# A fused spectral filter and feed-forward kernel: last transform stage placed by the chunk that needs it, filter sign moved to the prologue, half of batch 2's products by DMA exchange

## The chip, the cores and the metric

The kernel runs on one core of a Trainium2 chip. The metric is the device time of one launch in microseconds; lower is better. Times quoted as runs are launches timed on the device; the profile is one further execution recorded by the hardware profiler.

## The reference

Eight sequences of 3008 positions and 256 channels are filtered in the frequency domain, and the result goes through a two-layer network with a leaky ReLU.

```python
# x [8, 3008, 256], filt_r and filt_i [1505, 256], w_in [256, 2048], w_out [2048, 256]
X = np.fft.rfft(x, axis=1)
Y = X * (filt_r + 1j * filt_i)[None, :, :]
y = np.fft.irfft(Y, n=3008, axis=1).reshape(8 * 3008, 256)
h = y @ w_in
return np.maximum(0.01 * h, h) @ w_out
```

All inputs and the output are float32; the kernel computes its matmuls in float16 with float32 sums.

## The kernel before

**The transform.** The length 3008 is split into 94 x 32. For each sequence (called a batch, b = 0 to 7) the filter is four stages of matmuls with constant matrices. Each stage is cut into groups, and each group's matmuls fill one PSUM bank.

- Stage 1 (`s1_group`, matmul L218, 16 groups): transform over the 94 positions. ScalarE copies the bank out (for three quarters of batch 1's groups VectorE does), and SyncE's queue (SP) stores every second group to a DRAM scratch tensor `dz1` (L223). `t1_load` (L228) brings it back with rows and partitions exchanged, into a ring of four buffers `z1`.
- Stage 2 (`s2_group`, L264, 12 groups): transform over the 32 positions, with the twiddle factors in the matrix, and then the product with the filter. `fa_sb` holds the real part of the filter on all 128 partitions, `fb_sb` the imaginary part. Partitions 0 to 63 hold real rows and 64 to 127 imaginary ones, so that the product needs the halves exchanged. In general VectorE forms p2 = ps x fb (L273), two DMAs of 64 partitions each exchange its halves into p3 (L274, L275, on SP), VectorE forms p1 = ps x fa (L276), and GpSimd (POOL) adds p1 + p3 into y (L278). For batch 1 VectorE instead writes p3 directly with two operations of 64 partitions (L270, L271), so no DMA is needed. The tags p1, p2 and p3 have two buffers each, y has four.
- Stage 3 (`sa_group`, L284, 12 groups): inverse over the 32 positions, copied out by ScalarE (L286), stored to `dz2` (L288), and brought back by `t2_load` (L233) into the ring of four buffers `z2`.
- Stage 4 (`sb_group`, L302, 16 groups, two for each of the eight row blocks h): inverse over the 94 positions, copied by ScalarE (L294) into `yt`, the network's input.

Batch 0 goes through a prologue of its own (`first_s1` to `first_sb`), which uses VectorE transposes in the place of DRAM. There the upper half of `fb_sb` is a copy of the lower half (`upper`, L370), and the sign of the exchanged product is carried by the constant `inv2x`. Batch 1 takes the sign from a -1.0 in L270. After batch 1 the upper rows are negated in place (L569), and later batches need no sign.

**The network.** The 24064 rows are cut into 47 chunks of 512. `moe1` (L438) multiplies a chunk with w_in, and ScalarE applies the leaky ReLU (L443). In the first four chunks and the last one, the second product is `plain` (L541); in the others it is a seven-product scheme on quarters (`product`, L489), with VectorE sums of inputs (L466) and outputs (L513 to L533). Both use `out_banks`, two PSUM banks. `store` (L478) writes the output rows from SP's queue.

**The order.** Nothing reorders the work by itself. Every piece is put with a time on one heap and is issued in order of these times, to in-order engines and queues. One chunk has eight time units (`SL = 8`): its 16 `moe1` steps are half a unit apart, and the products of the chunk before are spread between them. `plan` gives each transform group its time: stage 1 at `s1 + s1_step * g`, stage 2 at `s2 + s2_step * g`, stage 3 `lag` later, stage 4 at `sb + sb_step * g`. The loads of x for the next batch go on POOL's queue at `s1 + xl + x_step * g`. The groups of all batches are then sorted and kept at least `GAP = 0.6` apart. The turned loads are placed three units ahead of their stage, but not sooner than 1.7 units after the last group of the stage before it. Steps that follow a group use `soon(delay, ...)`: the exchange DMAs one unit after stage 2, the POOL addition 3 units after it (1.2 in batch 1).

The transform groups share a ring of two PSUM banks (`single`, after one has been given to `out_banks`): a group waits until the group two places before it has been read out.

A stage 4 group of block h of batch b must come before the chunk that first reads the block, `QT * (8 * b + h) // CH` with QT = 376 and CH = 512; an assertion holds the plan to that.

Of the kernel before, what the change touches and what calls it, by code (L numbers as in the profile page):

```python
# [11 lines left out]
P = 128  # L12
FP16 = mybir.dt.float16
FP32 = mybir.dt.float32
AL = mybir.AluOpType
# [11 lines left out]
def _build_np_constants(N):  # L27
    n1, n2 = np.arange(N1), np.arange(N2)
    h = N2 // 2

    k2 = np.concatenate([np.arange(h), np.arange(N2 - 1, h - 1, -1)])

    sg = np.where(k2 < h, 1.0, -1.0)[None, :]
    th = 2 * np.pi * np.outer(n2, k2) / N2
    co, si = np.cos(th), np.sin(th)

    fwd1 = np.zeros((P, P))
    fwd2 = np.zeros((P, NC, P))
    inv1 = np.zeros((P, N2, N1))
    inv2 = np.zeros((P, P))  # L40

    for s, (qr, qi) in enumerate(((0, 2), (1, 3))):
        k1 = NC * s + np.arange(NC)

        cr, ci = (slice(64 * i + s, 64 * i + 64, 2) for i in range(2))
        r, i = (slice(Q * q, Q * q + Q) for q in (qr, qi))
        ang = 2 * np.pi * np.outer(n1, k1) / N1
        fwd1[:N1, qr * Q : qr * Q + NC] = np.cos(ang)
        fwd1[:N1, qi * Q : qi * Q + NC] = -np.sin(ang)
        for c in range(NC):  # L50
            t = th + 2 * np.pi * n2[:, None] * k1[c] / N
            fwd2[r, c, cr], fwd2[i, c, cr] = np.cos(t), np.sin(t)
            fwd2[r, c, ci], fwd2[i, c, ci] = -np.sin(t) * sg, np.cos(t) * sg

        w = np.where((k1 == 0) | (k1 == N1 // 2), 1.0, 2.0)[:, None] / N1
        for j in n2:
            t = ang.T + 2 * np.pi * j * k1[:, None] / N
            inv1[qr * Q : qr * Q + NC, j, :] = w * np.cos(t)
            inv1[qi * Q : qi * Q + NC, j, :] = -w * np.sin(t)
        inv2[cr, r], inv2[ci, r] = co.T, -(si * sg).T  # L60
        inv2[cr, i], inv2[ci, i] = si.T, (co * sg).T
    inv2 /= N2

    inv2x = np.concatenate([inv2[64:], -inv2[:64]], axis=0)
    small = np.stack([fwd1, inv2, inv2x], axis=1)

    fwd2t = fwd2.reshape(4, Q, NC, P).transpose(1, 0, 2, 3).reshape(P, NC, P)
    inv1t = inv1.reshape(4, Q, N2, N1)[:, :NC].transpose(1, 0, 2, 3).reshape(4 * NC, N2, N1)
    fwd2 = fwd2.reshape(P, FP, NC // FP, P).transpose(1, 0, 2, 3)
    return tuple(np.ascontiguousarray(t).astype(np.float16) for t in (fwd2, inv1, small, fwd2t, inv1t))  # L70
# [3 lines left out]
def kernel(  # L74
# [9 lines left out]
    nc = tc.nc  # L84
    B, N, D = x.shape
# [5 lines left out]
    CH = 512  # L91
    NCHUNK = TOK // CH
    assert NCHUNK * CH == TOK
    SL = 8
    NCH = NCT // 2
    QT = 4 * N1
    W0 = 4
    GAP = 0.6
    LANDED = 1.7
    SUMS = (0.9, 1.9, 2.9, 3.9)  # L100

# [11 lines left out]
    fa_sb = cpool.tile([P, NC, D], FP16, name="fa_sb")  # L113
    fb_sb = cpool.tile([P, NC, D], FP16, name="fb_sb")
# [21 lines left out]
    def bank(kind, n, w):  # L136
        of = wide if kind == "ph" else single
        t = of[turn[kind] % len(of)]
        turn[kind] += 1
        return t[:, : n * w].rearrange("p (n w) -> p n w", n=n)  # L140
# [5 lines left out]
    def at(time, f):  # L146
        clock["n"] += 1
        heapq.heappush(work, (time, clock["n"], f))

    def soon(delay, f):  # L150
        at(clock["now"] + delay, f)
# [3 lines left out]
    fwd1, inv2, inv2x = (small_sb[:, i, :] for i in range(3))  # L155
# [104 lines left out]
    def s2_group(b, g):  # L260
        def go():
            ps = bank("pf", 2, D)
            for j in range(2):
                nc.tensor.matmul(ps[:, j, :], f2_sb[:, 2 * g + j, :],  # L264
                                 z1[g // 2 % 4][:, 2 * (g % 2) + j, :],
                                 start=True, stop=True)
            fa, fb = fa_sb[:, ds(2 * g, 2), :], fb_sb[:, ds(2 * g, 2), :]
            p1, p2, p3 = (scrp.tile([P, 2, D], FP32, tag=f"p{i}", name=f"p{i}_b{b}_g{g}") for i in (1, 2, 3))
            if b == 1:
                nc.vector.scalar_tensor_tensor(p3[0:64], ps[64:P], -1.0, fb[64:P], AL.mult, AL.mult)  # L270
                nc.vector.tensor_tensor(p3[64:P], ps[0:64], fb[0:64], AL.mult)  # L271
            else:
                nc.vector.tensor_tensor(p2[:], ps, fb, AL.mult)  # L273
                soon(1, lambda: nc.sync.dma_start(p3[0:64], p2[64:P]))  # L274
                soon(1, lambda: nc.sync.dma_start(p3[64:P], p2[0:64]))  # L275
            nc.vector.tensor_tensor(p1[:], ps, fa, AL.mult)  # L276
            ys[(b, g)] = y1 = ypp.tile([P, 2, D], FP16, tag="y", name=f"y_b{b}_g{g}")
            soon(1.2 if b == 1 else 3, lambda: nc.gpsimd.tensor_tensor(y1[:], p1[:], p3[:], AL.add))  # L278
        return go

    def sa_group(b, g):
# [14 lines left out]
    def sb_group(b, g, copy):  # L296
        h, dt = g // 2, g % 2

        def go():
            ps = bank("pf", 4, N1)  # L300
            for j in range(4):
                nc.tensor.matmul(ps[:, j, :], z2[h % 4][:K4, j, ts(dt, P)], i1_sb[:K4, 4 * h + j, :],  # L302
                                 start=True, stop=True)
            quad_copy(h, dt, ps, copy)
        return go
# [3 lines left out]
    act, dve = nc.scalar.copy, nc.vector.tensor_copy  # L309
# [59 lines left out]
    def upper(hf, t, copy):  # L369
        copy(t[64:P, :, ts(hf, DH)], t[0:64, :, ts(hf, DH)])  # L370


    def keep_warm(n):
        for _ in range(n):
# [4 lines left out]
    g = 0  # L379
    for (n0, nn), fill in zip(first_parts, (4, 3, 1, 14)):  # L380
        while nn:
            n = 2 if nn % 4 or n0 >= N2 - 4 else 4
            first_s1(n0, n, two[n // 4], (dve, act)[g % 2])
            n0, nn, g = n0 + n, nn - n, g + 1
        keep_warm(fill)
    t1_part(0, 0, True)(), t1_part(0, 1, True)()
    upper(0, fa_sb, act), upper(0, fb_sb, dve)
    first_s2(0, 8, 8, "ph", True)
    t1_part(0, 2, True)()
    first_s2(0, 0, 8, "ph")  # L390
# [6 lines left out]
    t1_part(0, 3, True)()  # L397
    first_s2(0, 20, 4, "pf")
    upper(1, fa_sb, act)
    upper(1, fb_sb, dve)  # L400
    keep_warm(4)
    first_s2(1, 8, 8, "ph", True)
    first_s2(1, 0, 8, "ph")
# [12 lines left out]
    for g in range(8, 16):  # L416
# [6 lines left out]
    out_banks = [t[:].rearrange("p (a t d) -> p a t d", a=2, t=2)  # L423
                 for t in (psp_last, po_ps.rearrange("p a d -> p (a d)"))]
# [43 lines left out]
    done = {"products": 0}  # L468
# [68 lines left out]
    def plain(ci):  # L537

        def one(tj, ct):
            po = out_banks[tj % 2].rearrange("p a t d -> p (a t d)")[:, :D]  # L540
            nc.tensor.matmul(po, gts[ci][:, ct, ts(tj, P)], w_out_sb[:, ct, :],  # L541
                             start=(ct == 0), stop=(ct == NCT - 1))
            if ct < NCT - 1:
                return
            ot = outp.tile([P, D], FP32, tag="ost", padded_shape=[P, 6 * P], name=f"ost_c{ci}_t{tj}")
            (nc.vector.tensor_copy if ci < W0 else nc.scalar.copy)(ot[:], po)
            soon(0.5, lambda: store(ci, tj, ot[:]))
        return [lambda tj=tj, ct=ct: one(tj, ct) for tj in range(4) for ct in range(NCT)]

    groups, loads = [], []  # L550

    def plan(b, s1, s1_step, s2, s2_step, lag, sb, sb_step, xl, x_step):
        for g in range(16):
            groups.append((s1 + s1_step * g, 1, b, g, s1_group(b, g, dve if b == 1 and g % 4 < 3 else act)))
            if g % 2 and b + 1 < B:
                at(s1 + xl + x_step * g, lambda n0=2 * g - 2: x_load(b + 1, n0, 4))
        for c in range(6):
            loads.append((s2 - 3, 1, b, c, t1_load(b, c)))
        for g in range(12):
            groups.append((s2 + s2_step * g, 2, b, g, s2_group(b, g)))  # L560
            groups.append((s2 + lag + s2_step * g, 3, b, g, sa_group(b, g)))
        for h in range(8):
            loads.append((sb - 3, 3, b, h, t2_load(b, h)))
        for g in range(16):
            groups.append((sb + sb_step * g, 4, b, g, sb_group(b, g, act)))

    for i, (o, i0, i1) in enumerate(wt_sums):
        at(10 + 0.5 * i, lambda o=o, i0=i0, i1=i1: nc.vector.tensor_tensor(o, i0, i1, AL.subtract))
    at(32, lambda: nc.vector.tensor_scalar(fb_sb[64:P], fb_sb[64:P], -1.0, None, AL.mult))  # L569
    at(26, lambda: nc.sync.dma_start(i1_sb[:K4], i1t_d.ap()))  # L570
    plan(1, 0.3, 0.55, 13, 1.25, 3.3, 36.4, 2.94, 4, 1.6)
    plan(2, 13, 1.55, 43.5, 2.6, 6, 82.5, 2.94, 11, 2.2)
    plan(3, 42, 1.75, 75, 3.75, 6, 129, 2.94, 4, 2.94)
    for b in range(4, B):
        z = 47 * b
        plan(b, z - 121, 2.94, z - 69.5, 3.92, 6.5, z - 12, 2.94, 4, 2.94)

    last, when = -1, {}
    for time, stage, b, g, f in sorted(groups, key=lambda v: v[0]):
        last = max(time, last + GAP)  # L580
        when[stage, b, g] = last
# [3 lines left out]
    for time, stage, b, c, f in loads:  # L585

        after = when[stage, b, 15 if stage == 1 else 11] + LANDED
        at(max(time, after, place.get((stage, c % 4), 0)), f)
# [50 lines left out]
```

## Time and profile before

| what | value |
|---|---|
| runs | 761.75, 763.34, 763.74 us (median 763.34) |
| profiled execution | 761.49 us; span 759.7 us from its first to its last instruction |
| instructions | 18968 |
| TensorE matmul busy | 741.3 us (98%), granted clock 0.996 |
| ScalarE busy | 562.4 us (74%) |
| VectorE busy | 490.6 us (65%) |
| POOL busy | 169.2 us (22%) |
| DMA | 111.71 MB, 147 GB/s in the mean |

In the profile, PE is TensorE's matmuls, PEld its weight loads, DVE VectorE, ACT ScalarE. A row of the timeline gives start, duration, engine, line, operation, output<-inputs and shapes, and in brackets the idle time of the engine just before and what ended it. "x16" says that so many like instructions are merged. A row of the busy time by window gives the stretch, its length, and for each engine its busy time and instructions; then the granted TensorE clock, the DMA engines' busy share and GB/s. Matmuls are pipelined, and the recorded ends are modelled, so that records of successive matmuls overlap.

### The profile page before, as it was taken

What the parts mean: (1) busy time and instruction counts of PE and PEld (TensorE: products, weight loads), DVE (VectorE), ACT (ScalarE), POOL (GpSimd) and SP (SyncE); (2) the same over time, 40 slices, a digit from 0 to 9 for tenths busy, and PEclk for the clock granted to TensorE, in tenths of its full rate; (3) what the DMA queues carried; (4) which work ended last, traced back from release to release, by engine and by line L of the source; (5) the groups of instructions that cost most, each with busy time, mean ns of one, the idle gap of its engine ahead of it and who ended that gap; (6) DMA issues with size and microseconds to landing.
All of it is one profiled execution on the core that took longest, in us unless ns stands there. A gap on an engine that the chain in (4) does not pass through costs nothing.

```text
span 759.7 us, 18968 instructions
## 1 busy us (share of the span) xinstructions
PE 741.3 (98%) x7829; PEld 529.4 (70%) x7829; DVE 490.6 (65%) x665; ACT 562.4 (74%) x755; POOL 169.2 (22%) x171
## 2 busy tenths in 40 slices
PE   8899989999899999999999999999999999999997
PEld 3556657667577777877778777787677777777776
DVE  5866645767566687766766776677577676555561
ACT  4876777788687877777877877878777777666763
POOL 4703431242312221212223212212211210000000
PEclk9999999999999999999999999999999999999999
DMA  9996776777775578566775655544553433211012
GB/s 187 245 208 159 166 173 178 197 180 196 193 209 148 118 202 219 137 144 157 194 193 136 163 166 165 149 136 119 149 174 102 121 86 105 57 54 54 28 47 67
DMA packets 118726, 111.71 MB, mean 147 GB/s; under 512 B 16160, under 2 KB 92576, under 8 KB 118448
## 3 DMA queue, kind: packets, MB, share of 16 engines
q1 hardware_dynamic: 103776, 94.02, 41.9%
q0 software_dynamic: 14864, 16.49, 15.6%
q8 instruction: 61, 1.00, 0.5%
q14 instruction: 25, 0.20, 0.1%
HBM read 57.48 MB, written 50.33 MB: 142 GB/s over the span
## 4 chain that ended last, share of the span: by engine, by line
PE 75%; DMA 2%; DVE 1%; ACT 0%; SPq 0%; issue 0%; DVEq 0%
PE ph L438 35%; PE pf L489 16%; PE po_ps L489 16%; PE pf L302 2%; PE pf L218 2%; PE pf L264 2%; PE pf L284 2%; DMA dz<-big 1%; DMA big<-dz 1%; PE pf L541 0%; PE po_ps L541 0%; ACT gt_c L443 0%; SPq L478 0%; DVE p_b_g L273 0%; DVE ost_c_h L513 0%
## 5 line engine op out<-in xcount | busy, mean ns | idle before, releaser
L443 ACT ACTIVATE gt_c<-ph 128x1024 f16<-128x1024 f32 x376 | 385.4, 1025 | 141.8 <-PE ph L438 133.2
L438 PE MATMUL ph<-yt,w_in_sb 128*128 128x512 f16 (+7 forms) x1728 | 447.4, 351 | 0.7 <-ACT yt L294 0.7
L489 PEld LDWEIGHTS <-gt_c 128*128 128x128 f16 x2688 | 194.5, 98 | 90.3 <-issue 1.3
L278 POOL TENSOR_TENSOR y_b_g<-p_b_g,p_b_g 128x512 f16<-128x512 f32 x84 | 116.9, 1392 | 440.8 <-DMA p_b_g<-p_b_g 311.1
L489 PEld LDWEIGHTS <-big 128*128 128x128 f16 x2016 | 144.5, 98 | 62.1 <-issue 1.0
L438 PEld LDWEIGHTS <-w_in_sb 128*128 128x128 f16 x1728 | 138.3, 98 | 19.0 <-issue 0.9
L273 DVE TENSOR_TENSOR p_b_g<-pf,fb_sb 128x512 f32<-128x512 f32 x72 | 49.6, 689 | 44.5 <-PE pf L264 24.5
L221 ACT CAST big<-pf 128x512 f16<-128x512 f32 x100 | 58.2, 582 | 13.2 <-PE pf L218 11.6
L489 PE MATMUL po_ps<-wt_sb,gt_c 128*128 128x128 f16 x672 | 67.6, 219 | 0.3 <-DVE ost_c_h L513 0.3
L489 PE MATMUL pf<-wt_sb,gt_c 128*128 128x128 f16 x672 | 67.2, 219 | 0.3 <-DVE ost_c_h L513 0.2
L489 PE MATMUL pf<-w_out_sb,gt_c 128*128 128x128 f16 x672 | 64.3, 219 | 0.0
L489 PE MATMUL po_ps<-wt_sb,big 128*128 128x128 f16 x672 | 63.8, 219 | 0.0
L489 PE MATMUL po_ps<-w_out_sb,gt_c 128*128 128x128 f16 x672 | 63.8, 219 | 0.0
L294 ACT CAST yt<-pf 128x376 f16<-128x376 f32 x117 | 55.1, 474 | 11.3 <-PE pf L302 9.1
L489 PE MATMUL pf<-wt_sb,big 128*128 128x128 f16 x672 | 63.5, 219 | 0.0
L276 DVE TENSOR_TENSOR p_b_g<-pf,fa_sb 128x512 f32<-128x512 f32 x84 | 57.3, 682 | 0.6 <-POOL y_b_g L278 0.2
L466 DVE TENSOR_TENSOR gt_c<-gt_c 128x2048 f16<-128x2048 f16 x42 | 55.6, 1324 | 1.1
L466 DVE TENSOR_TENSOR big<-gt_c,big 128x2048 f16<-128x2048 f16 x42 | 55.9, 1332 | 0.0
L286 ACT CAST big<-pf 128x512 f16<-128x512 f32 x84 | 49.0, 583 | 5.8 <-PE pf L284 4.6
L466 DVE TENSOR_TENSOR big<-gt_c 128x2048 f16<-128x2048 f16 x42 | 52.1, 1240 | 0.2 <-ACT gt_c L443 0.2
L466 DVE TENSOR_TENSOR big<-big,gt_c 128x2048 f16<-128x2048 f16 x42 | 51.5, 1226 | 0.0
L541 PEld LDWEIGHTS <-gt_c 128*128 128x128 f16 x320 | 31.2, 98 | 18.5 <-issue 1.2
(85 smaller groups left out, 665.5 us busy)
## 6 DMA issues: line engine op xcount, KB each, us to landing
dz<-big SPq DMA_DIRECT2D x98, 256.0 KB
p_b_g<-p_b_g SPq DMA_DIRECT2D x144, 128.0 KB
out_dram<-ost_c_h SPq DMA_DIRECT2D x114, 128.0 KB
big<-dz SPq DMA_DIRECT2D x42, 256.0 KB
big<-dz SPq DMA_DIRECT2D x56, 192.0 KB
x_sb<-in_x_dram POOLq DMA_DIRECT2D x41, 192.0 KB, 4.5
out_dram<-ost_c_t SPq DMA_DIRECT2D x14, 128.0 KB
x_sb<-in_x_dram POOLq DMA_DIRECT2D x2, 768.0 KB, 10.0
```

The costliest lines, as they stand in the source:

```text
L218: nc.tensor.matmul(ps, fwd1[:N1], x_sb[:N1, ds(2 * g, 2), :], start=True, stop=True)
L221: copy(st[:, ds(2 * (g % 2), 2), :], ps)
L273: nc.vector.tensor_tensor(p2[:], ps, fb, AL.mult)
L276: nc.vector.tensor_tensor(p1[:], ps, fa, AL.mult)
L278: soon(1.2 if b == 1 else 3, lambda: nc.gpsimd.tensor_tensor(y1[:], p1[:], p3[:], AL.add))
L286: nc.scalar.copy(st2[h % 4][:, ds(2 * (g % 2), 2), :], ps)
L294: copy(yv, ps.rearrange("p c a -> p a c"))
L438: nc.tensor.matmul(ph[:, j, ds(t - ci * CH, e - t)], w_in_sb[:, dt, ts(ct, P)], yt[:, dt, ds(t % N, e - t)], start=(dt == 0), stop=(dt == ...
L443: nc.scalar.activation(gts[ci][:, ds(2 * g, 2), :], ph, AF.Lrelu)
L466: nc.vector.tensor_tensor(o, i0, i1, op)
L489: nc.tensor.matmul(po[:, t], a()[:, c, ts(t, P)], w[:, c, :], start=(c == 0), stop=(c == NCH - 1))
L541: nc.tensor.matmul(po, gts[ci][:, ct, ts(tj, P)], w_out_sb[:, ct, :], start=(ct == 0), stop=(ct == NCT - 1))
```

## The change

- The prologue's copy into the upper half of `fb_sb` becomes a multiplication by -1 (`minus`); the later negation (L569) is gone, and `inv2x` has the opposite sign in its second half.
- In batch 1, the even groups of stage 2 keep the direct products, now with a plain `tensor_tensor` in the place of the scaled one. The odd groups use the DMA exchange as other batches do, with the POOL addition 2.6 units after stage 2.
- A stage 4 group is placed at its planned time or, where that is earlier, 3.5 units (first of a block's two groups) or 1.5 units (second) before the chunk that needs the block.
- `plain` takes its output bank by the count of products made. The count is read when the step is issued, after all the product lists have been made; it is 295 then, so that the first tile of a plain chunk uses the second bank.
- The plan's numbers change for batches 1, 2 and 4 to 7.

```diff
-    inv2x = np.concatenate([inv2[64:], -inv2[:64]], axis=0)
+    inv2x = np.concatenate([inv2[64:], inv2[:64]], axis=0)
...
+    EXG = 0
...
-            if b == 1:
-                nc.vector.scalar_tensor_tensor(p3[0:64], ps[64:P], -1.0, fb[64:P], AL.mult, AL.mult)
+            if b == 1 and g % 2 == EXG:
+                nc.vector.tensor_tensor(p3[0:64], ps[64:P], fb[64:P], AL.mult)
                 nc.vector.tensor_tensor(p3[64:P], ps[0:64], fb[0:64], AL.mult)
             else:
                 nc.vector.tensor_tensor(p2[:], ps, fb, AL.mult)
...
-            soon(1.2 if b == 1 else 3, lambda: nc.gpsimd.tensor_tensor(y1[:], p1[:], p3[:], AL.add))
+            soon(1.2 if b == 1 and g % 2 == EXG else 3 if b > 1 else 2.6, lambda: nc.gpsimd.tensor_tensor(y1[:], p1[:], p3[:], AL.add))
...
+    def minus(o, i):
+        nc.vector.tensor_scalar(o, i, -1.0, None, AL.mult)
...
-    upper(0, fa_sb, act), upper(0, fb_sb, dve)
+    upper(0, fa_sb, act), upper(0, fb_sb, minus)
...
-    upper(1, fb_sb, dve)
+    upper(1, fb_sb, minus)
...
-            po = out_banks[tj % 2].rearrange("p a t d -> p (a t d)")[:, :D]
+            po = out_banks[(done["products"] + tj) % 2].rearrange("p a t d -> p (a t d)")[:, :D]
...
-            groups.append((sb + sb_step * g, 4, b, g, sb_group(b, g, act)))
+            due = SL * (QT * (8 * b + g // 2) // CH)
+            groups.append((min(sb + sb_step * g, due - 3.5 + 2 * (g % 2)), 4, b, g, sb_group(b, g, act)))
...
-    at(32, lambda: nc.vector.tensor_scalar(fb_sb[64:P], fb_sb[64:P], -1.0, None, AL.mult))
...
-    plan(1, 0.3, 0.55, 13, 1.25, 3.3, 36.4, 2.94, 4, 1.6)
-    plan(2, 13, 1.55, 43.5, 2.6, 6, 82.5, 2.94, 11, 2.2)
+    plan(1, 0.3, 0.55, 12.8, 1.25, 3.3, 37, 2.8, 4, 1.6)
+    plan(2, 13, 1.55, 43.5, 2.6, 5.5, 84.2, 2.8, 13, 2.3)
...
-        plan(b, z - 121, 2.94, z - 69.5, 3.92, 6.5, z - 12, 2.94, 4, 2.94)
+        plan(b, z - 121, 2.94, z - 69, 3.92, 6.5, z - 11.6, 2.94, 4, 2.94)
```

## The prediction

> **What bounds the kernel now.** The page came first, then busy time by window, then TensorE's waits and, around each long one, the timeline.
>
> ```profile
> PE 741.3 (98%) x7829; PEld 529.4 (70%) x7829; DVE 490.6 (65%) x665; ACT 562.4 (74%) x755; POOL 169.2 (22%) x171
> ```
> ```profile
> 39.00:120.00 81.00, 78.03 (x512) 48.30 (x510) 44.37 (x72) 57.75 (x74) 22.85 (x25) 1.00 0.77 178
> 120.00:210.00 90.00, 85.50 (x931) 60.46 (x928) 61.69 (x85) 71.30 (x100) 26.21 (x27) 1.00 0.76 188
> 210.00:740.00 530.00, 528.79 (x5976) 389.53 (x5974) 352.90 (x474) 401.60 (x535) 96.57 (x88) 1.00 0.49 133
> ```
>
> After the span, the first column is TensorE: from 210 to 740 us it is idle for 1.2 us, from 39 to 210 for 7.5 us. TensorE is in order, so only its idle time can shrink. Its records overlap, so I took each start-to-start interval less the median of its kind (216 ns for 512 columns, 56 ns for the L489 products). From 39 us to the end 12.4 us of excess remain, nearly all at these places:
>
> ```profile
> 203.32 0.33 PE L489 MATMUL po_ps<-w_out_sb,gt_c 128*128 128x128 f16 x3
> 206.26 0.35 PE L302 MATMUL pf<-i_sb,big 96*128 96x94 f16 x4 [2.61 <-DMA big<-dz]
> ```
> ```profile
> 113.61 0.35 PE L302 MATMUL pf<-i_sb,big 96*128 96x94 f16 x4 [1.89 <-DMA big<-dz]
> ```
> ```profile
> 166.75 0.38 PE L438 MATMUL ph<-yt,w_in_sb 128*128 128x512 f16 x1 [0.69 <-ACT yt L294]
> ```
> ```profile
> 748.48 1.91 PE L541 MATMUL pf<-w_out_sb,gt_c 128*128 128x256 f16 x16 [0.52 <-DVE ost_c_h L513]
> ```
>
> By excess: 2.78 us where batch 2's last stage waits for its first turned load, 2.05 where batch 1's does, 0.85 where chunk 8 waits for batch 1's yt, 0.85 at 542.5 (batch 7's stage 2, its load late), 0.68 at the end (the plain product wants the bank that the last product's VectorE addition is leaving), 1.72 in seven waits of batch 1 (one row above all: the two-bank ring still held by VectorE), 1.04 at 143.3 (ring, VectorE late), 0.59 at batch 1's first load; the rest small.
>
> The chain of waits gives the largest:
>
> ```profile
> 196.48 0.87 ACT gt_c L443
> 197.35 6.22 DMA dz<-big
> 203.59 2.63 DMA big<-dz
> ```
>
> The store to DRAM takes 6.22 us, the load back 2.63. And batch 1's products:
>
> ```profile
> L270 DVE SCALAR_TENSOR_TENSOR p_b_g<-pf,fb_sb x12: 692/693/694, 59.3 to 97.9; 64x512 f32<-64x512 f32 x12
> L271 DVE TENSOR_TENSOR p_b_g<-pf,fb_sb x12: 683/683/685, 60.0 to 98.7; 64x512 f32<-64x512 f32 x12
> L276 DVE TENSOR_TENSOR p_b_g<-pf,fa_sb x12: 692/692/692, 60.7 to 99.4; 128x512 f32<-128x512 f32 x12
> ```
>
> Half the partitions cost the full time. A direct group holds its bank 2.5 us from its matmul, an exchanged one (two operations) 1.9.
>
> **The skill.** "VectorE: DVE Perf Modes", The perf-mode tier table, puts tensor_copy and tensor_scalar in one tier on 16-bit SBUF data. The trace agrees: the 64x3072 copies take 996 ns, the 64x6144 negation 1873. "DMA: Bandwidth & Descriptors", Anatomy of one DMA, gives a fixed cost of about 2 us. The exchange's second issue to its POOL addition takes 1.9 us at least, median 3.6 and at most 5.8 in batch 2: the fixed part is there, and more under load. The same page, Issuing engines are not separate DMA queues, says that they share the 16 engines. In agreement, three x loads (about 580 KB) are on POOL's queue at 104-110, just when batch 1's store takes 4.5 us.
>
> **The change, part by part.** The order of TensorE's work follows from the plan's numbers (due times, then the 0.6 spacing), so I listed it for both versions; listed so, the old order fits the trace matmul for matmul. "Distance" below is TensorE work between two points, without waits.
>
> 1. Negation. L370 on VectorE becomes a multiplication by -1, twice, at 996 ns either way (bounds -0.1, +0.1); L569's 1.87 us at 101.2 goes, VectorE being idle around it. L270's scalar_tensor_tensor becomes tensor_tensor, 693 to 683 ns. The sign of inv2x is data. Zero.
>
> 2. Batch 2's last stage: plan 82.5 to 84.2, lag 6 to 5.5. Last stage-3 group to first stage-4 group was 8.08 us apart plus 2.78 waiting, so the chain needs 10.86. The new distance is 12.08. The load (at start - 3, now 81.2) moves past SP's intervening work, but still ahead of the store's landing. -2.8; bounds -2.8 and -0.5. The shorter lag cuts stage 2 to 3 of group 11, already 0.42 late, by 0.17: +0.2.
>
> 3. Placement by chunk. For group 9 of batch 1 the distance to chunk 8 grows from 0.57 to 1.06 us (crowding eats the rest), so 0.85 becomes about 0.35: -0.5. Elsewhere the least leads are 1.8 us (batch 4) and 2.1 (batch 2); evacuation took 0.85 to 1.6 from the matmul. Zero; at worst +0.5.
>
> 4. Batches 4 to 7: stage 2 later by 0.5, stage 4 by 0.4. Batch 7's load was issued at 539.89 behind output stores on SP. It stays behind them, but its matmul is 0.82 us later in the order: -0.8. Batch 5's load moves past the stores at 2.8 into a chunk; it had 8.4 us of lead against some 3, so it hides. Other SP meetings may open: 0 to +1.5, I take 0.
>
> 5. Plain banks. At the end the parity frees the first tile: -0.7. In the first chunks it makes chunk 3's last tile share the first product's bank. That tile's copy ends at 119.26, the product starts at 119.08: +0.25.
>
> 6. x loads of batch 3: start +2.1 units, step 2.3. Two of the three at 104-110 leave batch 1's store window. I take -0.4 from the 2.05; bounds -1.0, 0. Their users are 6 units later, so their delay hides. Batch 1's stage 2 at 12.8 arrives 0.1 us earlier at its load: +0.1.
>
> 7. Exchange in six odd groups. VectorE saves 6 x 0.69 us; of the seven ring waits those behind odd groups go, while direct groups 4, 6, 8 and 10 keep the 2.4 us distance that cost about 0.28: 1.1 instead of 1.72, -0.6. Added are 12 DMAs of 128 KB on SP, issued in 1.1 us a pair; SP's plan point (+1 unit, about 2 us) is after the product is ready at 1.2, so nothing queues behind a waiting exchange for long. POOL's addition waits instead, and behind it x loads and the next direct addition (about 5 us of slack before). The chain is 0.48 to VectorE, 0.69, issue 1.16, landing, addition 1.27 and handover: 3.7 us plus landing. Batch 2 shows 5.85 to 12.3, median 7.6. Distances in batch 1 are 7.7, 9.0, 10.2, 9.0, 8.7 and 6.3 us (groups 1 to 11). Group 11 waits whenever landing exceeds 2.6 us; over batch 2's twelve values the mean excess is 1.2. Its successor's distance is unchanged, so this adds to the 2.05. Groups two apart share p1, so VectorE waits for POOL when landing exceeds about 4; with group 1 that is some 0.7. +1.9; bounds 0 and +6.
>
> Sum: -2.8 + 0.2 - 0.5 - 0.8 - 0.7 + 0.25 - 0.4 + 0.1 - 0.6 + 1.9 = -3.35 us, from the profiled span of 759.7 to about 756.3. That execution was timed at 761.49, the lower end of the runs; from the median 763.34 the same loss gives 760.0.
>
> **Rivals.** *The exchange becomes the bound* (slower): all odd chains at 10 us, inside batch 2's values, cost 2.3 + 1.0 + 0 + 1.0 + 1.3 + 3.7 = 9.3 us on TensorE against 5.3 of gains: +4, 767. For it: batch 1 has the tightest distances and DMA at 77%. Against: the distances were 2.6 to 5.3 us longer than the direct chain, and five of six exceed batch 2's median. It decides from a mean chain of about 9 us.
> *The wait only moves* (no change): batch 2's store is slowed by traffic moved beside it, or SP reaches the load late, and only 1 us of 2.8 comes back, with the exchange at its estimate: -1.5, 761.8. For it: 6.2 us against batch 1's 4.5 shows how the store varies.
> *The exchange hides*: landing near 2 us, as in batches 4 to 7 (median 2.0). Then item 7 is -0.6 and the gain 5.2: 758.1. Against: DMA is 77% busy here, 49% there.
> *The change doesn't do what it says*: placement by chunk hardly binds, since the spacing sets most groups; that costs item 3 alone.
>
> **How the numbers follow.** About 0.3%, or 2.3 us, can be told from no change. The forecast (gain 2.3 to 5) has 0.57, the hidden exchange 0.10, the moved wait 0.21, the slower rival 0.12. The likeliest gives 760.0. The range 757.2 to 763.8 runs from the hidden exchange plus half of item 6's bound past the moved wait to the start of the slower rival; about 0.05 lies below and 0.12 above. Faster 0.67, same 0.21, slower 0.12.
>
> **What would show it.** Right: no wait over 0.5 us at batch 2's first L302; none at the last L541; batch 1's odd chains of 6 to 9 us and a wait of about 1 us before its last L284; SP's load for batch 7 before need. Wrong: waits at L284 or on VectorE behind POOL adding up to over 4 us between 60 and 105; a store over 7 us behind batch 2's last stage; new waits past 210.

## The result and the profile after

The changed kernel takes 757.71 us in the median of six runs (756.39 to 759.59); the kernel before takes 762.07 us over six runs, three of them taken beside the change. The ratio is 0.9944, 95% interval 0.9924 to 0.9964: a gain of about 0.6%. Ratios and intervals here are those on record; they are close to the quotients of the medians, but not the same. The forecast was 760.0 us with a range of 757.2 to 763.8, and most likely faster; the measured time lies in the lower part of that range. The profiled execution, timed at 758.15 us, spans 756.4 us, 3.3 less than before's.

Batches are counted from 0: the products of which half now go by exchange are those of batch 1, the second sequence, which the title calls batch 2.

The change adds lines, so that numbers move: L218 is now L219, L264 L265, L284 L285, L302 L303, L438 L442, L466 L470, L489 L493, L541 L545, L478 L482; the exchange is L275 and L276, the POOL addition L279. The busy time by window of the changed kernel, columns as before (length, then TensorE first):

```profile
39.00:120.00 81.00, 77.68 (x514) 48.45 (x512) 38.03 (x64) 58.02 (x75) 21.01 (x24) 1.00 0.81 195
120.00:210.00 90.00, 88.39 (x960) 62.59 (x958) 64.25 (x87) 73.92 (x104) 25.12 (x27) 1.00 0.80 201
210.00:740.00 530.00, 527.19 (x5963) 388.58 (x5961) 350.10 (x473) 400.87 (x533) 95.27 (x89) 1.00 0.49 132
```

Between 120 and 210 us TensorE's idle time falls from 4.5 us to 1.6. Between 39 and 120 it is 3.3 against 3.0. From 210 to 740 us it rises from 1.2 to 2.8. Outside these stretches it falls from 5.2 to 4.5 us ahead of 39 us and from 4.6 to 3.6 us behind 740. So most of the gain was made in one stretch, and part of it was lost again past 210 us, where the prediction expected a gain. VectorE's 44.4 us in the first stretch became 38.0.

The timeline's TensorE rows at the places of before:

```profile
205.79 0.34 PE L303 MATMUL pf<-i_sb,big 96*128 96x94 f16 x4
```
```profile
112.99 0.35 PE L303 MATMUL pf<-i_sb,big 96*128 96x94 f16 x4 [1.94 <-DMA big<-dz]
```
```profile
166.19 0.59 PE L442 MATMUL ph<-yt,w_in_sb 128*128 128x512 f16 x2
```
```profile
744.71 1.06 PE L493 MATMUL pf<-w_out_sb,big 128*128 128x128 f16 x16
745.66 1.91 PE L545 MATMUL po_ps<-w_out_sb,gt_c 128*128 128x256 f16 x16
```

The first is batch 2's stage 4, with no bracket: its wait of 2.78 us is gone. Batch 1's stage 4 still waits. The third row is the start of chunk 8, which no longer waits for batch 1's yt. At the end the plain product now takes po_ps and follows the last product at once.

Two waits are new, at batch 4's last stage 3 group and at batch 6's stage 2:

```profile
368.28 0.38 PE L285 MATMUL pf<-y_b_g,small_sb 128*128 128x512 f16 x1 [1.73 <-POOL y_b_g L279]
```
```profile
453.48 0.39 PE L265 MATMUL pf<-big,f_sb 128*128 128x256 f16 x2 [1.05 <-DMA big<-dz]
```

Measured as in the prediction (start-to-start interval less its kind's median), waits from 39 us on, in us:

| place | before | after |
|---|---|---|
| batch 1, first stage 2 | 0.59 | 0.73 |
| batch 1, ring behind direct groups | 1.72 (seven) | 1.17 (four) |
| batch 1, exchange of group 1 | - | 0.36 |
| batch 1, stage 4 | 2.05 | 2.11 |
| chunk 3's last tile to chunk 4's first product | 0 | 0.24 |
| ring at 143 | 1.04 | 1.11 |
| chunk 8 for batch 1's yt | 0.85 | 0 |
| batch 2, last stage 3 | 0.42 | 0.83 |
| batch 2, stage 4 | 2.78 | 0 |
| batch 4, last stage 3 | 0 | 1.90 |
| batch 6, stage 2 | 0 | 1.22 |
| batch 7, stage 2 | 0.85 | 0 |
| last plain product | 0.68 | 0 |
| all, with small ones | 12.4 | 9.9 |

The waits account for 2.5 us of the span's 3.3. The first L438 (now L442) starts 0.6 us earlier and the tail after the last matmul is 0.5 shorter; small differences between the two executions take the rest the other way.

### The profile page after: what moved, and what is told of

Same layout as the page of the kernel before. It is cut to its first block, busy times and chain, and to the rows that moved or that the text cites. A ratio compares the mean times of both kernels' runs of the same rounds, so it can differ in the third digit from the quotient of the medians.

```text
span 756.4 us, 18976 instructions
## 1 busy us (share of the span) xinstructions
PE 740.5 (98%) x7829; PEld 529.5 (70%) x7829; DVE 483.1 (64%) x658; ACT 563.0 (74%) x755; POOL 165.0 (22%) x171
## 4 chain that ended last, share of the span: by engine, by line
PE 88%; DMA 5%; DVE 3%; ACT 2%; issue 1%; POOL 1%; SPq 0%; DVEq 0%; POOLq 0%; ACTq 0%
PE ph L442 39%; PE pf L493 17%; PE po_ps L493 17%; PE pf L219 3%; PE pf L303 3%; PE pf L265 2%; PE pf L285 2%; DMA p_b_g<-p_b_g 2%; DMA big<-dz 2%; PE po_ps L545 1%; PE pf L545 1%; PE po_ps L379 1%; DMA dz<-big 1%; PE pf L349 1%; POOL y_b_g L279 1%
## 5 line engine op out<-in xcount | busy, mean ns | idle before, releaser
L442 PE MATMUL ph<-yt,w_in_sb 128*128 128x512 f16 (+7 forms) x1728 | 447.2, 351 | 0.0
L493 PEld LDWEIGHTS <-gt_c 128*128 128x128 f16 x2688 | 194.3, 98 | 91.6 <-issue 2.8
L279 POOL TENSOR_TENSOR y_b_g<-p_b_g,p_b_g 128x512 f16<-128x512 f32 x84 | 114.0, 1358 | 443.8 <-DMA p_b_g<-p_b_g 309.5
L493 PEld LDWEIGHTS <-big 128*128 128x128 f16 x2016 | 144.8, 98 | 61.8 <-issue 1.1
L442 PEld LDWEIGHTS <-w_in_sb 128*128 128x128 f16 x1728 | 138.1, 98 | 19.7 <-issue 1.0
L274 DVE TENSOR_TENSOR p_b_g<-pf,fb_sb 128x512 f32<-128x512 f32 x78 | 53.7, 689 | 51.8 <-PE pf L265 31.5
L493 PE MATMUL pf<-wt_sb,gt_c 128*128 128x128 f16 x672 | 67.5, 219 | 0.0
L493 PE MATMUL po_ps<-wt_sb,gt_c 128*128 128x128 f16 x672 | 67.4, 219 | 0.0
L493 PE MATMUL po_ps<-wt_sb,big 128*128 128x128 f16 x672 | 64.8, 219 | 0.0
L493 PE MATMUL pf<-wt_sb,big 128*128 128x128 f16 x672 | 64.0, 219 | 0.0
L493 PE MATMUL po_ps<-w_out_sb,gt_c 128*128 128x128 f16 x672 | 63.9, 219 | 0.0
L493 PE MATMUL pf<-w_out_sb,gt_c 128*128 128x128 f16 x672 | 63.5, 219 | 0.1
L470 DVE TENSOR_TENSOR gt_c<-gt_c 128x2048 f16<-128x2048 f16 x42 | 54.5, 1297 | 1.1
L470 DVE TENSOR_TENSOR big<-gt_c,big 128x2048 f16<-128x2048 f16 x42 | 54.9, 1308 | 0.0
L470 DVE TENSOR_TENSOR big<-big,gt_c 128x2048 f16<-128x2048 f16 x42 | 52.7, 1256 | 0.0
L470 DVE TENSOR_TENSOR big<-gt_c 128x2048 f16<-128x2048 f16 x42 | 52.1, 1241 | 0.2 <-ACT gt_c L447 0.2
L219 PE MATMUL pf<-x_sb,small_sb 94*128 94x512 f16 x112 | 42.7, 381 | 1.1 <-DVE p_b_g L277 0.9
## 6 DMA issues: line engine op xcount, KB each, us to landing
x_sb<-in_x_dram POOLq DMA_DIRECT2D x2, 768.0 KB, 10.1
```

Source lines behind the costliest of these rows:

```text
L219: nc.tensor.matmul(ps, fwd1[:N1], x_sb[:N1, ds(2 * g, 2), :], start=True, stop=True)
L279: soon(1.2 if b == 1 and g % 2 == EXG else 3 if b > 1 else 2.6, lambda: nc.gpsimd.tensor_tensor(y1[:], p1[:], p3[:], AL.add))
L442: nc.tensor.matmul(ph[:, j, ds(t - ci * CH, e - t)], w_in_sb[:, dt, ts(ct, P)], yt[:, dt, ds(t % N, e - t)], start=(dt == 0), stop=(dt == ...
L470: nc.vector.tensor_tensor(o, i0, i1, op)
L493: nc.tensor.matmul(po[:, t], a()[:, c, ts(t, P)], w[:, c, :], start=(c == 0), stop=(c == NCH - 1))
```

## The experiments

Theory at the outset: TensorE's waits are distances missing in the order of issue. The change bought distance for batch 2's stage 4, chunk 8 and the end. The late waits come from the new times of batches 4 to 7, and the exchange is about neutral. Rivals: the exchange is what pays, or what costs; the late waits are chance.

| kernel | median, us | ratio to before, 95% interval |
|---|---|---|
| e1, batch 1 direct | 758.78 | 0.9977, 0.9963 to 0.9991 |
| e2, old late times | 756.37 | 0.9940, 0.9923 to 0.9957 |
| e3, placement and batch 2 alone | 758.27 | 0.9958, 0.9946 to 0.9969 |
| e4, late times alone | 762.34 | 1.0016, 1.0003 to 1.0029 |
| e5, changed kernel again | 757.41 | 0.9951, 0.9934 to 0.9969 |
| e6, all exchanged | 762.99 | 1.0026, 1.0015 to 1.0036 |
| e7, old late times and direct | 757.66 | 0.9949, 0.9930 to 0.9967 |
| e8, combination | 755.87 | 0.9926, 0.9906 to 0.9946 |
| e9, old late times, batch 1's stage 4 later | 754.34 | 0.9919, 0.9895 to 0.9943 |
| e10, the same, direct | 755.73 | 0.9933, 0.9907 to 0.9958 |
| e11, stages 2 and 3 late | 757.36 (one run) | |
| e12, stage 4 late | 756.71 (one run) | |

The kernel before had medians of 761.41 beside e1 to e4, 761.57 beside e5 to e8 and 760.88 beside e9 to e12.

**e1: the exchange undone in the changed kernel.**

```diff
-            if b == 1 and g % 2 == EXG:
+            if b == 1:
...
-            soon(1.2 if b == 1 and g % 2 == EXG else 3 if b > 1 else 2.6, lambda: nc.gpsimd.tensor_tensor(y1[:], p1[:], p3[:], AL.add))
+            soon(1.2 if b == 1 else 3, lambda: nc.gpsimd.tensor_tensor(y1[:], p1[:], p3[:], AL.add))
```

> The changed kernel with batch 1's odd groups direct again, so with no exchange in batch 1. Theory (the exchange is about neutral: it bought 0.55 us of ring waits and cost 0.36 at group 1): ring waits between 58 and 105 us back to about 1.7 us from 1.2, the 0.36 at 69 us gone, time within 0.5 us of the changed kernel, so 4 us below the kernel before. Rival (the exchange is what pays): time back by over 1.5 us. Rival (the exchange costs, as predicted, 1.9): over 1 us faster than the changed kernel.

Ring waits are back at 1.75 us (plus 0.30 at group 10) and the exchange wait is gone, as the neutral theory says. But the wait before batch 1's stage 4 is 2.55 us, and after it TensorE runs at half clock for 3.4 us, which costs some 1.5 us more. Neither theory had this mechanism. This execution, timed at 762.12 us, is one of the slowest of its 22 (756.64 to 762.13), so that the median holds less of it: 1.1 us above the changed kernel's, with intervals that just touch. The late waits (1.89 and 1.61) appear at the same two places.

**e2: the changed kernel with the old times of batches 4 to 7.**

```diff
-        plan(b, z - 121, 2.94, z - 69, 3.92, 6.5, z - 11.6, 2.94, 4, 2.94)
+        plan(b, z - 121, 2.94, z - 69.5, 3.92, 6.5, z - 12, 2.94, 4, 2.94)
```

> The changed kernel with the old times of batches 4 to 7 (stage 2 at z - 69.5, stage 4 at z - 12). Theory (the new waits of 1.90 us before batch 4's last stage 3 group and 1.22 us before batch 6's stage 2 come from the shifted times, the loads meeting other traffic on SP and the DMA engines): both go, the 0.85 at batch 7's stage 2 comes back, net 2.2 us faster than the changed kernel. Rival (they are chance of one execution): waits of this size appear elsewhere, time within 1 us of the changed kernel.

Both late waits are gone and batch 7's is back at 0.51; waits of 7.2 us remain in all. The profiled span is 753.6 us, 2.8 below the changed kernel's. In the runs the median is 1.3 us below it, and the intervals overlap widely, so that the waits and not the times show what the late stages cost.

**e3: placement by chunk and batch 2's new numbers in the kernel before.**

```diff
-            groups.append((sb + sb_step * g, 4, b, g, sb_group(b, g, act)))
+            due = SL * (QT * (8 * b + g // 2) // CH)
+            groups.append((min(sb + sb_step * g, due - 3.5 + 2 * (g % 2)), 4, b, g, sb_group(b, g, act)))
...
-    plan(2, 13, 1.55, 43.5, 2.6, 6, 82.5, 2.94, 11, 2.2)
+    plan(2, 13, 1.55, 43.5, 2.6, 5.5, 84.2, 2.8, 11, 2.2)
```

> The kernel before with placement by chunk and batch 2's new lag and stage 4 times (5.5, 84.2, 2.8), nothing else. Theory (the 2.78 us at batch 2's first L302 are bought by these two together): that wait is zero, the wait at batch 2's last L284 up from 0.42 to about 0.7, the 2.05 of batch 1 and the 0.85 before chunk 8 stay (lead 0.57 us), time 2.3 us below the kernel before. Rival (the store or load simply grows with the later place): the wait stays at 1 us or more, time within 1 us of before.

The timeline at batch 2's stage 4:

```profile
206.51 0.33 PE L489 MATMUL pf<-wt_sb,gt_c 128*128 128x128 f16 x3
206.68 0.34 PE L302 MATMUL pf<-i_sb,big 96*128 96x94 f16 x4
```

There is no wait, while 0.85 before chunk 8 and 2.02 at batch 1 stay. One part of the expectation failed: no wait is left at batch 2's last L284. These two edits alone give a ratio of 0.9958. They need each other: with batch 2's new numbers and no placement by chunk, the plan puts group 7 of batch 2 at 104.1, while its chunk begins at 104.

**e4: only the new late times, in the kernel before.** The diff is e2's read the other way.

> The kernel before with only the new times of batches 4 to 7 (z - 69, z - 11.6). Theory (shifted times open new waits): the 0.85 at batch 7's stage 2 is gone, about 1.9 at batch 4's last stage 3 group and 1.2 at batch 6's stage 2 appear, time 2 us above the kernel before. Rival (as predicted, only batch 7's wait goes): 0.8 us below it. Rival (chance): waits at places that the changed kernel does not show.

Slower than before by 0.03 to 0.29%, so the direction of the theory holds. Batch 7's wait is gone, batch 6's stage 2 waits 0.45, and batch 4's last stage 3 group only 0.12, its addition ending just in time (0.05 us). The sizes don't hold, and in this profile what came is less than what went, so that it doesn't show where the time was lost. Batch 2's stage 4, which lies ahead of everything that the edit moves, waits 2.32 us here, and a stretch at half clock follows that too.

**e5: the changed kernel again.**

> The changed kernel once more, for a second profile beside the following kernels. Theory (the waits are set by the order of issue): the same waits as in its first profile, 1.9 us before batch 4's last stage 3 group, 1.2 before batch 6's stage 2, 2.1 before batch 1's stage 4, none at batch 2's stage 4 or at the end; ratio to the kernel before about 0.9955. Rival (chance): the two late waits move or go.

The late waits stand at the same places, smaller: 0.72 and 0.65. Batch 2's stage 4 and the end have none. Batch 1's stage 4 waits only 0.62. So places follow from the order, and sizes vary by more than 1 us between executions.

**e6: all of batch 1's groups exchanged**, twice the suspected cost.

```diff
-    EXG = 0
+    EXG = 2
...
-            soon(1.2 if b == 1 and g % 2 == EXG else 3 if b > 1 else 2.6, lambda: nc.gpsimd.tensor_tensor(y1[:], p1[:], p3[:], AL.add))
+            soon(1.2 if b == 1 and g % 2 == EXG else 3 if b > 1 else 2.4, lambda: nc.gpsimd.tensor_tensor(y1[:], p1[:], p3[:], AL.add))
```

> The changed kernel with all of batch 1's groups exchanged (addition at 2.4 units). Theory (ring waits behind direct groups go, the exchange's landing of 2 to 4 us is covered where the distance is 8.7 us or more): the four ring waits (1.17 us) go, groups 0 and 1 wait 0.5 to 1.5 us in all, time within 1 us of the changed kernel. Rival (as in the prediction, the exchange becomes the bound: 12 more DMAs of 128 KB and chains of 9 to 10 us): 3 to 8 us of waits before L285 between 60 and 105 us, time 3 us or more above the changed kernel.

The rival won in its time (some 5.6 us above the changed kernel run beside it, e5), with 1.25 us at group 1 and this at group 8:

```profile
97.04 0.38 PE L285 MATMUL pf<-y_b_g,small_sb 128*128 128x512 f16 x1 [2.03 <-DVE p_b_g L277]
97.25 0.99 PE L442 MATMUL ph<-yt,w_in_sb 128*128 128x512 f16 x2
98.04 1.06 PE L545 MATMUL pf<-w_out_sb,gt_c 128*128 128x256 f16 x4
```

Group 8's chain took 10.1 us, since its DMAs were issued 2.9 us after its product, SP standing at output stores ahead of them. Its addition held p1, group 10's product waited for that on VectorE until 96.29 and so kept its bank, and L285 needed the bank. The two L442 matmuls after it take 0.79 us instead of 0.43: half clock, here and again after 2.80 us at batch 1's stage 4.

**e7: old late times and batch 1 direct** (e1's and e2's edits together).

> The changed kernel with the old times of batches 4 to 7 and batch 1 all direct. Theory (the exchange is about neutral): ring waits 1.7 us against 1.25, time within 0.7 us of the exchanging kernel with the old late times, ratio to before about 0.9945. Rival (the exchange pays 2 us or more, as the lone undoing of it seemed to show, 0.9977 against 0.9944): ratio about 0.997.

The time agrees with the neutral theory (a ratio of 0.9949 against e2's 0.9940, the intervals overlapping). The profile shows the same ring waits and, again, a longer wait at batch 1's stage 4, 3.66 us, with half clock after it. By window (the granted clock stands after the five engines):

```profile
100.00:115.50 15.50, 12.04 (x78) 7.22 (x75) 1.80 (x4) 10.72 (x16) 2.74 (x4) 1.00 0.69 160
115.50:120.00 4.50, 4.33 (x25) 2.53 (x26) 0.42 (x1) 1.52 (x3) 0.00 (x0) 0.62 0.64 199
120.00:125.00 5.00, 4.92 (x47) 3.47 (x46) 2.19 (x3) 3.31 (x4) 0.00 (x0) 1.00 0.31 94
```

The clock falls to 0.62 in the mean just after the wait and is full again at 120 us.

**e8: distance for batch 1's stage 4, old times for batches 4 to 6, the new stage 2 for batch 7.**

```diff
+            time = 38.3 + 0.9 * g if b == 1 and g < 2 else min(sb + sb_step * g, due - 3.5 + 2 * (g % 2))
-            groups.append((min(sb + sb_step * g, due - 3.5 + 2 * (g % 2)), 4, b, g, sb_group(b, g, act)))
+            groups.append((time, 4, b, g, sb_group(b, g, act)))
...
-        plan(b, z - 121, 2.94, z - 69, 3.92, 6.5, z - 11.6, 2.94, 4, 2.94)
+        plan(b, z - 121, 2.94, z - (69 if b == 7 else 69.5), 3.92, 6.5, z - 12, 2.94, 4, 2.94)
```

> The changed kernel with the old times of batches 4 to 6, the new stage 2 time for batch 7 alone (its stage 4 at the old time), and batch 1's first two stage 4 groups at 38.3 and 39.2. Theory (waits are distances missing in the order): batch 1's L303 has 1.96 us more distance, so its wait falls from about 2 us to below 0.3, unless chunk 5 then waits for the second group (lead 1.26 us) by up to 0.4; batch 7's wait is gone, none at batches 4 and 6; 1.5 to 2.5 us below the kernel with the old late times alone, ratio to before about 0.9915. Rival (the load simply ends later): batch 1's wait stays above 1.5 us.

Batch 1's wait is gone and chunk 5 doesn't wait. But batch 7's stage 2 now waits 1.35 us: the new time doesn't help it here. Only part of the expected gain over e2 came (0.9926 against 0.9940, the intervals overlapping).

**e9: e8 with the old time for batch 7 too.**

> The changed kernel with the old times of batches 4 to 7 and batch 1's first two stage 4 groups at 38.3 and 39.2. Theory (waits are missing distance): no wait at batch 1's stage 4 (1.7 in the kernel with old late times), about 0.5 at batch 7's stage 2 (1.35 with the new time there), none at batches 4 and 6: waits of about 5.5 us in all, ratio to the kernel before about 0.9915. Rival (chance sets what is left): another wait of 1 us or more appears, ratio 0.993 or above.

```profile
113.26 0.49 PE L545 MATMUL pf<-w_out_sb,gt_c 128*128 128x256 f16 x3
113.76 0.35 PE L303 MATMUL pf<-i_sb,big 96*128 96x94 f16 x4
```

Waits of 6.2 us in all, 0.17 at batch 1's stage 4 and 0.48 at batch 7. One of 0.85 us at batch 2's first stage 2 is new. The lowest median of all, 754.34 us, below both kernels; its interval overlaps the changed kernel's.

**e10: e9 with batch 1 direct.**

> The same with batch 1 all direct. The wait before batch 1's stage 4 has 2 us of spare distance here, so the exchange is seen by itself. Theory (exchange neutral in itself): ring waits 1.7 us against about 1.25 plus 0.3 of exchange waits, time within 0.7 us of the kernel that exchanges, no stretch at half clock near 115 us. Rival (the exchange pays by itself): over 1.5 us slower although no wait precedes batch 1's stage 4. Rival (direct groups delay batch 1's store): a wait of 1 us or more at batch 1's stage 4 in spite of the distance.

```profile
115.19 0.35 PE L303 MATMUL pf<-i_sb,big 96*128 96x94 f16 x4 [1.75 <-DMA big<-dz]
```

The third expectation came true: 1.92 us of wait in spite of 2 us more distance. No half clock follows. The time is 1.4 us above e9's. The intervals of the ratios overlap, but the runs themselves, taken beside each other, are nearly apart: 753.98 to 755.41 us (six) for e9, 754.90 to 757.22 (seven) here.

**e11 and e12: the late times taken apart.** e11 has z - 69 with z - 12, e12 z - 69.5 with z - 11.6.

> The changed kernel with only stage 2 and 3 of batches 4 to 7 late (z - 69), stage 4 at z - 12. Theory (batch 5's load of 1 MB, put at 163.0, falls behind the stores at 162.8 and straight ahead of the exchange of batch 4's last group at 163.6): a landing of 5 us or more for that exchange and a wait of 0.7 to 1.9 us before batch 4's last stage 3 group; 0.5 to 1.6 us at batch 6's stage 2. Rival (stage 4's later times do it): no such waits.

> The changed kernel with only stage 4 of batches 4 to 7 late (z - 11.6), stage 2 at z - 69.5. Theory (the load's place does it): landing of 2 us for the exchange of batch 4's last group, no wait there or at batch 6's stage 2, about 0.5 at batch 7's stage 2. Rival (stage 4's later times do it): waits of 0.7 us or more at batches 4 and 6.

The waits at batches 4 and 6 are 0.44 and 1.40 in e11 and absent in e12. These are single executions, but all six profiles with the late stage 2 in batches 4 to 7 have both waits (0.12 us and more), and none of the eight others has either. So stage 2's time makes them. Batch 4's in e11:

```profile
367.13 0.38 PE L285 MATMUL pf<-y_b_g,small_sb 128*128 128x512 f16 x1 [0.27 <-POOL y_b_g L279]
```

SP's queue, e11 and then e12:

```profile
355.92 1.78 SPq L482 DMA_DIRECT2D out_dram<-ost_c_h  x2
357.80 1.82 SPq L229 DMA_DIRECT2D big<-dz  x4
359.73 0.53 SPq L275 DMA_DIRECT2D p_b_g<-p_b_g  x1
360.30 0.59 SPq L276 DMA_DIRECT2D p_b_g<-p_b_g  x1
```
```profile
352.81 3.29 SPq L229 DMA_DIRECT2D big<-dz  x4
356.53 2.38 SPq L482 DMA_DIRECT2D out_dram<-ost_c_h  x3
359.01 0.53 SPq L275 DMA_DIRECT2D p_b_g<-p_b_g  x1
359.60 1.47 SPq L276 DMA_DIRECT2D p_b_g<-p_b_g  x1
```

In e11 batch 5's load, four DMAs of 256 KB, stands right ahead of the exchange of batch 4's last group. From the end of the exchange's second issue to the POOL addition that needs it, the landing, 4.92 us pass. In e12 the load is 6 us ahead and the landing takes 1.99. All kernels with the late stage 2 in all four batches agree: the changed kernel (5.43), e1 (5.52), e4 (3.36), e5 (5.20) and e6 (5.75); those with the old one, e2, e3, e7 to e10 and the kernel before, have about 2.

The size of batch 4's wait follows the addition too: it takes 2.23, 2.23 and 1.89 us in the three executions that wait 1.9 us (the changed kernel, e1, e6), and 1.27 in those that wait 0.72, 0.44 and 0.12 (e5, e11, e4). VectorE's sums (L470) and POOL's addition in the changed kernel:

```profile
365.88 1.23 DVE L470 TENSOR_TENSOR big<-gt_c 128x2048 f16<-128x2048 f16 x1
366.00 2.23 POOL L279 TENSOR_TENSOR y_b_g<-p_b_g,p_b_g 128x512 f16<-128x512 f32 x1 [12.50 <-DVE ost_c_h L525]
367.14 2.17 DVE L470 TENSOR_TENSOR gt_c<-gt_c 128x2048 f16<-128x2048 f16 x1
```

The addition ends 1.11 us after the first sum, and the second sum 1.09 us after the addition. Alone they take 1.27 and 1.22 us, so the two took turns. All 13 additions over 1.4 us in this profile overlap such a sum. In e5 the addition came first, at 364.79, and the sum at 364.90 took 2.25 us. So about 1 us of batch 4's wait hangs on which of the two starts first.

Batch 7's stage 2 waits 1.69 us in e12, against 0.30 to 0.85 in the others with its old stage 2 time, which these runs don't explain.

## Why the prediction was right, point by point

The sum of -3.35 us on the span met 3.3, and the direction and the range held. That the sum met is in part luck. The waits that it is made of fell by 2.5 us, and the rest came from an earlier first chunk and a shorter tail, which the prediction put at nothing. Among the waits, batches 4 to 7 were forecast 3.1 us too well and the exchange 1.5 us too badly, which cancelled by half. Of the signs of being wrong that it named, one came: new waits past 210 us. Of the signs of being right, the wait of about 1 us before batch 1's last stage 3 group did not come. The lower end of its range doesn't follow from its own terms either: 758.1 less half of item 6's bound of 1.0 is 757.6, not 757.2.

1. *Negation, zero.* The two multiplications took 0.95 and 1.37 us in the changed kernel, the two copies 0.95 and 1.04 before, and no cost of it shows further on. The first L442 came at 38.2 to 39.0 us in the eleven profiles with the new prologue, and the first L438 at 38.9 to 39.2 in three with the old. In the changed kernel's profile the first multiplication itself already starts 0.7 us earlier than the copy did, so that its earlier first chunk is not the negation's doing.
2. *Batch 2's last stage, -2.8.* Right. The wait is zero in the changed kernel and in every experiment with its numbers; e3 shows it alone. The side cost of the shorter lag was sized 0.2 and was 0.41 in this profile, where the last to come was the exchange's addition, and 0 in e3.
3. *Placement, -0.5.* The size was under, 0.85 went, and the cause was another. e3 has the placement and keeps the 0.85. By the plan's arithmetic group 9 of batch 1 stands at 63.5 before and in e3, and at 63.4 in the changed kernel, with the placement or without it. So it is batch 1's new stage 4 numbers that move it, ahead of chunk 7's last `moe1` step at 63.5. Before, ScalarE copied its bank only behind the leaky ReLU of that step:

```profile
165.32 1.02 ACT L443 ACTIVATE gt_c<-ph 128x1024 f16<-128x1024 f32 x1 [0.36 <-PE ph L438]
166.24 0.47 ACT L294 CAST yt<-pf 128x376 f16<-128x376 f32 x1
```

In the changed kernel the copy, at 164.47, comes ahead of it, and the distance to chunk 8 is 2.10 us, not 1.06. No run has these numbers alone. The other step that failed is the sentence that placement hardly binds and costs item 3 alone if it did nothing. It makes the later start of item 2 possible at all.
4. *Batches 4 to 7, -0.8.* Wrong in sign, the term with the greatest error: batch 7's 0.85 went, and 1.90 and 1.22 came, +2.3 net. The failed step is "it hides": batch 5's load hid itself, its own stage 2 being in time, but the exchange behind it did not. The prediction had asked who waits for the moved load, not what is queued behind it. At batch 6 the late stage 2 makes the wait (e11 against e12): its load lasts about 7 us, when before's had landed within 6.0. In all six profiles with the late stage 2, POOL issues a pair of x loads 0.7 us ahead of this load, in the eight others at least 3.5 us ahead. That they slow it fits, but no run has it alone, and the cause stays open. Nor is batch 7's gain the simple shift of the forecast: in e8, with batch 7 alone late, it waits 1.35 us.
5. *Banks, -0.7 and +0.25.* Right: 0.68 went. Chunk 3's last copy ends at 118.65 us, the first product starts at 118.70, 0.24 later than its kind follows.
6. *x loads, -0.4.* Not seen in this profile (2.05 to 2.11). Over the five profiles whose first 115 us have the changed kernel's plan (it, e2, e5, e11, e12) the wait is 0.62 to 2.11, mean 1.5, so the value may hold in the mean. With direct groups the moved loads went with a longer store: 5.7 to 6.1 us from issue to the load behind it (e1, e7, e10), where it was 4.7 to 4.9 with the old x times (before, e3, e4) and 3.7 to 4.9 with half the groups exchanged.
7. *Exchange, -0.6 and +1.9.* The ring's part was right: four waits behind direct groups, 1.17 us. The cost was mis-sized: 0.36 against 1.9, and 0.3 to 1.0 over the seven profiles with the same plan there (at group 1 or group 9). Group 11, charged 1.2, never waited in the changed kernel, as its exchange landed in 2.19 us; batch 2's distribution was the wrong row for it. The slower rival was real but needs twice the exchanges (e6): it decided by shared p1 buffers, as priced, and by SP's stores ahead of the exchange, which the prediction had not priced. The exchange's worth by itself is near nothing; what it does for batch 1's store is larger (e1, e7 and e10 against the changed kernel, e2 and e9), and that link is shown in the profiles without its mechanism being settled. The section on the anatomy of one DMA that the prediction cites describes DMAs issued from GpSimd. The exchange is issued from SP, so that its least landing, 1.9 us, rests on the trace alone.

The timed gain, 4.4 us, exceeds the spans' 3.3. A stretch at half clock after batch 2's wait, as in e4, would add to some runs of the kernel before. The record fits this: of the 59 runs of before beside e1 to e4, the 20 with a granted clock of 0.995 or less have a median of 762.57 us, the 39 others 760.58. Where in these runs the clock fell isn't known, so it is argued, not shown.

## What to carry to other kernels

When an in-order engine is nearly full, list its order of issue with the distances in work, and compare each with the chain that must fit: this gave the large wait, the bank waits and the end to a few tenths. For every DMA that a new time moves, ask what is queued right behind it: one megabyte of loads was itself in time, and the 256 KB exchange that came next then cost up to 1.9 us, about 1 us of it by an addition that had to take turns with VectorE. Moving a stage later may need another rule, here placement by its consumer, before the plan allows it.

## What was not expected of the hardware

TensorE's clock. The Trainium skill, "TensorE: Matmul & The Clock Gate", What's actually happening, speaks of half clock after an idle window of about 3.4 us, counted by free-running windows. Here, past the prologue, six waits were of 2.19 to 3.66 us. Five of them (e1, e4, e6 twice, e7) were followed by one stretch of 3.4 us at a granted clock of 0.5; before's 2.78 us was not, and no wait of 2.11 us or less was. By window, first the kernel before behind its 2.78 us, then e6 behind its two waits:

```profile
206.00:211.00 5.00, 4.74 (x52) 3.41 (x53) 2.71 (x5) 2.89 (x4) 1.18 (x3) 1.00 0.91 179
```
```profile
97.00:101.00 4.00, 3.96 (x16) 2.15 (x16) 0.84 (x2) 1.60 (x2) 1.51 (x2) 0.57 0.97 159
117.00:122.00 5.00, 5.00 (x30) 3.10 (x28) 0.42 (x1) 2.42 (x4) 0.00 (x0) 0.66 0.66 200
```

The clock records of the traces show the windows themselves. In e1, e4 and e7 the stretch starts 27, 53 and 27 times 3.413 us after the half-clock stretch of the prologue (in e1 at 114.62 and 22.46 us), and e6's two start six times 3.413 us apart (97.31 and 117.79). Laid on this grid, each of the five waits left TensorE idle for 2.19 to 3.09 us within the one window just ahead of the stretch. Before's wait, from 203.49 to 206.26, is cut by a boundary at 204.85 into 1.37 and 1.41 us. The most that any window between the first chunk and the last matmul held without such a stretch after it is 2.01 us (e3). So in these fourteen profiles the idle time within one window tells the two cases apart, with a limit between 2.01 and 2.19 us of the 3.41. The window's length and that it runs free agree with the page; that it need not be idle throughout is what the runs add. In e1, e6 and e7 each stretch adds some 1.5 to 1.7 us to the matmul intervals behind it. So an idle time that grows from 2.0 to 2.5 us may cost 2 us where it falls into one window, and only the 0.5 where a boundary cuts it.
